# Two P V products of chunks 2 to 4 put directly behind each other, first W2 pieces and LayerNorm moved

## The chip, the cores and the metric

The kernel runs on one core of one Trainium2 chip. The metric is the device time of one execution in microseconds (us). A second measure is the span of the profiled execution: from its first to its last instruction. TensorE (PE in the profile; PEld for its weight loads) does the matrix products, VectorE (DVE), ScalarE (ACT) and GpSimd (POOL) the element-wise work, SyncE (SP) issues nearly all transfers.

## The reference

Two branches are computed from the same LayerNorm and added to the input:

```python
x = A_x                                   # [1, 2048, 576], bf16
xn = _layernorm(x, axis=-1)               # no scale, no shift, eps 1e-5
return x + _A_ref(xn, A_wqkv, A_wo) + _B_ref(xn, B_w1, B_w3, B_w2)
# _A_ref: 32 heads of 18, causal attention, each query sees the last 256 keys
#   scores = q k^T * 18**-0.5; p = softmax over the window; o = p v; o @ wo
# _B_ref: h = silu(xn @ w1) * (xn @ w3), 4608 wide; h @ w2
```

## The kernel before

The 2048 tokens are worked in four chunks of 512 (c = 0 to 3 in the code, chunks 1 to 4 in the text). W1, W3 and W2 are streamed from memory again for every chunk. The heads are taken in groups of four (g = 0 to 7) and pairs of groups (j = 0 to 3).

A chunk has these stages, one behind the other on TensorE:

1. **36 units** (u = 0 to 35; `unit_pairs`, L851). A unit makes 128 of the 4608 hidden features: nine steps (n = 0 to 8) of two matmuls of 64 rows each, one for W3 and one for W1, into two PSUM banks. `unit_tanh` (L866, ScalarE) and `unit_h` (L872, two VectorE instructions) then make `hT[:, u]`. Three pairs of banks (`JOBS`, dealt by `job()`) take turns, so unit u+3 writes where unit u was read.
2. Between the steps of the units stands attention: **score steps** (`score_step`, L1357: matmuls of L682, the exponential L691, masks L718) and **P V** (`pv`, L721: matmuls of 20 columns by 64 rows, L739). Chunk 1 does all eight groups here, chunks 2 to 4 groups 4 to 7 (pairs 2 and 3: 20 score steps, 96 matmuls for each P V). A P V writes two banks that `job()` gives it; `pv_out` (L799) turns them on VectorE, `o_scale` (L802) divides by the row sums, `o_turn` (L811) turns back, `o_pack` (L819) sends the result to `oT` by transfers.
3. Projections for the next chunk (L496), and then W2 with the scores and P V of groups 0 to 3 of the next chunk between (`w2_lanes`, L958). Chunk 4 has W2 and Wo alone instead (`p2_item`, L918).

The order on every engine is written out by the program. The planner has a clock that counts steps: a unit's step is 1, a score step 1, a P V `PV_COST` = 6.6 (L1288). `spaced_step` (L1368) spreads the score steps so that they end at `last`, which was the end of the units less 26 in chunks 2 to 4. In chunks 2 to 4 pair 2 has its P V behind unit `LATE_PV` = 20 (L1290, L1439), pair 3 behind unit 35 (L1496; in chunk 4 L1546, behind the first Wo matmuls of L846). In chunk 1 pairs 1 and 2 are at `JOINT` = (27, 6) (L1291, L1402), that is before the seventh step of unit 27: both P V run directly behind each other, in the two pairs of banks that unit 27 does not use. `calm` (L1305) keeps score steps out of the eight steps before it.

The probabilities of a score step lie in a slot. The first ten slots of chunks 2 to 4 (`early`, L1322) are borrowed: four are tiles 28 to 35 of `hT`, four the buffers of W2, two are tiles of `stage`. So the first four pieces of W2 (`load_w2`, L366) can be loaded only once the P V of pair 2 has read them. They are asked for behind units 25, 27, 29 and 31 in chunks 2 to 4 and behind units 27 to 30 in chunk 1.

LayerNorm of the next chunk's four token tiles is spread over the units by `near` (L1302): statistics at unit 8+4t, `ln_apply` at 10+4t, the transposing transfer `xn_send` at 11+4t. The rows of x are loaded at units 1, 2, 12 and 15 (L1307). W1 and W3 of later units are loaded in parts behind units 3, 7, ..., 23 (`owe_part`, L355): each part is issued when the step n = 3 or n = 8 of the unit after that is through; SP works its transfers in the order of the program.

Of the kernel before, what the change touches and what calls it, by code (L numbers as in the profile page):

```python
# [164 lines left out]
def bass_parallel_sum__sliding_block__glu_gated_swiglu__prompt_kernel(  # L165
# [21 lines left out]
    NF = F // 128  # L187
# [10 lines left out]
    with ExitStack() as es:  # L198
# [166 lines left out]

        def load_w2(upto):  # L366
            nonlocal n2fill
            if n2fill >= min(upto, NC * 2 * NFC):
                return
            s = n2fill % NW2  # L370
            m = n2fill % (2 * NFC)
            half, fc = divmod(m, NFC)
            n2fill += 1
            if n2fill <= (NC - 1) * 2 * NFC:
                if m < 16:
                    dst, f0, nf, d0, nd = w2_by(s, 128), m % 4 * 9, 9, m // 4 * 128, 128
# [6 lines left out]
            add("sp", lambda e: e.dma_start(  # L383
                w2[s][:], B_w2[fc * 512:(fc + 1) * 512, half * HD:(half + 1) * HD].rearrange("(fl p) d -> p fl d", p=128)),
                w=[("w2", s)], dma=f"w2_{s}")

# [911 lines left out]
        for c in range(NC):  # L1298
# [13 lines left out]
            npv = 3 if c == 0 else 1  # L1312
            total = 9 * NF + len(att) + npv * PV_COST
            start = 60 if c == 0 else 8
            last = total - AHEAD[c]
            nxt = soon = start
# [22 lines left out]
            def later(u, what):  # L1339
                side.setdefault(u, []).append(what)  # L1340
# [27 lines left out]
            def spaced_step():  # L1368
                nonlocal nxt, soon, clock
                score_step()  # L1370
                soon = clock + 7.5
                room = last - clock - PV_COST * (3 - next_pv) - 5 * sum(v > at_u for v in xt)
                nxt = max(soon, clock + room / max(1, len(att) - done))
                clock += 1
# [17 lines left out]
            for u in range(NF):  # L1392
# [44 lines left out]
                if u % 4 == 3 and u < (NF - 4 if c + 1 == NC else NF - 12) and (c or u != 15) or c and u == 0:  # L1437
                    owed += 2 if c or u >= 11 else 4
                if u == (LATE_PV if c else FIRST):  # L1439
                    j = next_pv  # L1440
                    assert j == j0 and clock >= pv_ready[j], (c, clock, pv_ready)
                    next_pv += 1
                    banks = job()
                    pv(c, j, banks)
                    clock += PV_COST
                    if c == 0:
                        release(j, None)
# [5 lines left out]
                    if j == 0:  # L1453
                        for n in range(7):
                            later(u + 5 + n, lambda n=n: o_rest(n, "sp"))
                unit_h(u, b0[0])
# [35 lines left out]
            assert done == len(att) and next_pv == 3, (done, next_pv)  # L1492
            assert clock + 2 >= pv_ready[3], (clock, pv_ready)
            if c + 1 < NC:
                banks = job()
                pv(c, 3, banks)  # L1496
                for g in range(GN, G):
# [10 lines left out]
                for m, what in enumerate(PROJ_LATER + [None]):  # L1508
                    got = proj_begin(c + 1, what) if what else proj_end()
                    if m == 0:  # L1510
                        xn_swap(c + 1, ("sp", "sp"))
                        if c == 0:
                            wo_late()
                        for u in sorted(side):
                            for do in side.pop(u):
                                do()
                        pv_out(banks[0], 0)
                        pv_out(banks[1], 1)
                        o_scale(0)
                    elif m == 1:  # L1520
                        o_turn(6, 0)
                        o_turn(6, 1)
                        o_scale(1)
                    elif m == 2:
                        o_turn(7, 0)
                        o_turn(7, 1)
# [3 lines left out]
                    elif got and got[0] == "8":  # L1530
                        new_k(2)
                    if m == 6:
                        o_pack(3, "sp")
# [11 lines left out]
            wo_rest(0, True, False)  # L1545
            pv(c, 3, banks)  # L1546
            for n, item in enumerate(p2_list(c)):
                p2_item(c, item, xs)
                if n == 3:
                    for u in sorted(side):  # L1550
                        for what in side.pop(u):
                            what()
                    pv_out(banks[0], 0)
                    pv_out(banks[1], 1)
                    o_scale(0)
                    o_turn(6, 0)
                    o_turn(6, 1)
                    o_scale(1)
                    o_turn(7, 0)
                    o_turn(7, 1)  # L1560
                    o_pack(3, "act")

# [30 lines left out]
```

## Time and profile before

| | us |
|---|---|
| three runs | 554.01, 554.99, 555.89; median 554.99 |
| the profiled execution | 554.85 |
| its span, first to last instruction | 553.1 |
| outside of the span | 1.75 |

A line of the profile's groups names line, engine, operation, what it writes and reads, the shapes and the count; behind the bar come busy time, the mean of one in ns, and the idle time ahead of them with what ended it. Matmuls overlap, so a mean of 376 ns of a matmul with 512 columns doesn't mean that it takes the engine that long: two on different rows of the array run beside each other, and the next pair starts 0.216 us later. In the timeline a row is a run of like instructions: start, length, and the count behind the x. "issue" is what the profile says where an engine stood idle and nothing that the profile knows held it back.

### The profile page before, as it was taken

To read this page: it belongs to the slowest core of one execution; us is meant where nothing else is said; L and a number is where in the kernel's file an instruction comes from. 1 tells how busy PE (TensorE), PEld (TensorE's weight loads), DVE (VectorE), ACT (ScalarE), POOL (GpSimd) and SP (SyncE) were. 2 spreads that over 40 slices of the span, in tenths; PEclk is the share of its full clock that TensorE was granted. 3 is DMA by queue.
4 is the path that set the end of the run, shared out by engine and by line. 5 is a ranking of instruction groups with operands and counts; after the bars stand their busy time and mean duration, and the time that the engine had idled before them with its cause. 6 is when DMAs were issued, how large, how long until landed. Compare 5 with 4: busy or idle time off the path is not lost.

```text
span 553.1 us, 17657 instructions
## 1 busy us (share of the span) xinstructions
PE 548.0 (99%) x7690; PEld 301.7 (55%) x7690; DVE 365.2 (66%) x745; ACT 294.0 (53%) x481; POOL 120.0 (22%) x281
## 2 busy tenths in 40 slices
PE   8999999999999999999999999999999999999998
PEld 4555445465564444455556444446555644545776
DVE  6566888845748888673764888866466686677211
ACT  6457776268825555536883555443787355554000
POOL 5513544200012423200001232320000222221000
PEclk9999999999999999999999999999999999999999
DMA  9997999849799997945989999793587999881552
GB/s 237 198 208 143 192 200 158 168 97 163 143 180 192 190 187 147 179 98 115 151 142 195 198 189 190 145 176 79 119 163 143 180 195 163 167 175 54 140 151 64
DMA packets 166070, 88.12 MB, mean 159 GB/s; under 512 B 101546, under 2 KB 163754, under 8 KB 165994
## 3 DMA queue, kind: packets, MB, share of 16 engines
q1 hardware_dynamic: 164514, 85.27, 82.2%
q10 hardware_dynamic: 1480, 1.73, 1.3%
q8 instruction: 60, 0.98, 0.8%
q14 instruction: 16, 0.13, 0.1%
HBM read 71.30 MB, written 2.36 MB: 133 GB/s over the span
## 4 chain that ended last, share of the span: by engine, by line
PE 97%; DMA 1%; SPq 1%; POOL 0%; issue 0%; DVE 0%
PE ps L860 51%; PE ps L1036 17%; PE ps L496 8%; PE ps L932 6%; PE ps L682 4%; PE ps L739 2%; PE ps L1086 2%; PE ps L1045 2%; PE ps L791 2%; PE ps L756 1%; DMA pt<-in_A_wqkv_dram 1%; PE ps L939 1%; SPq L1168 0%; PE ps L1096 0%; SPq L1172 0%
## 5 line engine op out<-in xcount | busy, mean ns | idle before, releaser
L860 PE MATMUL ps<-xnT,w 64*128 64x512 bf16 x1400 | 177.5, 376 | 0.0
L860 PE MATMUL ps<-xnS,w 64*128 64x512 bf16 x1120 | 148.6, 376 | 0.0
L875 DVE SCALAR_TENSOR_TENSOR gs<-thb,ps 128x512 bf16<-128x512 bf16 x144 | 97.9, 680 | 66.1 <-ACT thb L869 65.6
L869 ACT ACTIVATE thb<-ps 128x512 bf16<-128x512 f32 x144 | 85.6, 595 | 58.9 <-PE ps L860 57.7
L1036 PE MATMUL ps<-hT,w 32*128 32x512 bf16 x1728 | 106.9, 374 | 0.0
L860 PEld LDWEIGHTS ps<-xnT,w 64*128 64x128 bf16 x1400 | 67.2, 94 | 71.6
L878 DVE SCALAR_TENSOR_TENSOR hT<-gs,ps 128x512 bf16<-128x512 bf16 x144 | 98.9, 687 | 5.0
L860 PEld LDWEIGHTS ps<-xnS,w 64*128 64x128 bf16 x1120 | 53.7, 94 | 57.3
L1036 PEld LDWEIGHTS ps<-hT,w 32*128 32x128 bf16 x1728 | 57.3, 92 | 29.2 <-issue 1.4
L763 ACT ACTIVATE pt<-ps 128x512 bf16<-128x512 f32 x120 | 65.1, 594 | 7.7 <-PE ps L756 7.5
L691 ACT ACTIVATE pt<-ps 128x1024 bf16<-128x1024 f32 (+1 forms) x46 | 46.2, 1005 | 42.2 <-PE ps L682 42.2
L756 PE MATMUL ps<-qv,kn 18*128 18x384 bf16 (+2 forms) x288 | 54.6, 267 | 0.0
L806 POOL TENSOR_TENSOR oq<-uq,rden 128x288 bf16<-128x288 f32 x15 | 10.1, 672 | 198.7 <-DVE rden L805 198.7
L718 POOL TENSOR_TENSOR pt<-pt,mk 128x128 int32<-128x128 int32 (+1 forms) x82 | 33.0, 423 | 69.4 <-ACT pt L691 69.4
L771 DVE TENSOR_TENSOR pt<-pt,kv 128x256 int32<-128x256 int32 x96 | 31.4, 372 | 24.8 <-ACT pt L763 24.2
L496 PE MATMUL ps<-xnT,wp 64*128 64x512 bf16 (+1 forms) x360 | 38.2, 355 | 0.4 <-POOL mk L1270 0.4
L932 PE MATMUL ps<-w,hT 128*128 128x288 bf16 (+1 forms) x292 | 36.9, 284 | 0.0
L691 ACT ACTIVATE hT<-ps 128x1024 bf16<-128x1024 f32 (+1 forms) x20 | 20.0, 1002 | 31.5 <-PE ps L682 31.4
L756 PEld LDWEIGHTS ps<-qv,kn 18*128 18x128 bf16 x288 | 26.5, 93 | 15.0 <-DVE uq L800 0.8
L932 PEld LDWEIGHTS ps<-w,hT 128*128 128x128 bf16 x292 | 28.2, 98 | 7.3 <-issue 0.2
L682 PE MATMUL ps<-qv,kv 64*128 64x320 bf16 (+4 forms) x336 | 31.7, 258 | 0.0
L813 DVE STREAM_TRANSPOSE od<-oq 128x256 bf16<-128x256 bf16 x64 | 25.2, 424 | 6.3 <-POOL oq L806 6.3
(128 smaller groups left out, 522.8 us busy)
## 6 DMA issues: line engine op xcount, KB each, us to landing
w<-in_B_w_dram SPq DMA_DIRECT2D x60, 576.0 KB, 7.8
w<-in_B_w_dram SPq DMA_DIRECT2D x72, 288.0 KB, 4.3
w<-in_B_w_dram SPq DMA_DIRECT2D x12, 192.0 KB, 6.5
xp<-in_A_x_dram SPq DMA_DIRECT2D x4, 576.0 KB, 4.6
xnS<-xnT SPq DMA_DIRECT2D x8, 256.0 KB, 5.3
xp<-in_A_x_dram SPq DMA_DIRECT2D x14, 144.0 KB, 4.3
w<-in_B_w_dram SPq DMA_DIRECT2D x6, 320.0 KB, 4.8
oT<-od SPq DMA_DIRECT2D x52, 36.0 KB
```

The source lines that it names most:

```text
L496: op = add("pe", lambda e, out_=out_, st=st, mv=mv, n=n, r0=r0, first=first: e.matmul(out_, st, mv, start=first, stop=(part == 1 and n == ...
L682: add("pe", lambda e, r0=r0, out_=out_, kb=kb, q0=q0, nb=nb: e.matmul(out_, kb4[r0:r0 + 64, g - GN, kb + NV - NB, :] if kb < 0 else kv[r0: ...
L691: add("act", lambda e: e.activation(pt_slot(sl)[:, 0:w, :], PS[:, SC[0]:SC[1] + 1, 0:w].rearrange("p r q -> p q r"), ACT.Exp, scale=scale) ...
L718: add("pool", lambda e, vb=vb, mm=mm: e.tensor_tensor(vb, vb, mm, ALU.mult), r=(key if n == 0 else []) + ["mk"], **{"w" if n == 0 else "j" ...
L756: add("pe", lambda e: e.matmul(PS[:, b, c0:c0 + nb * 128], kn[32 * a:32 * a + Dh, g, W + 128 * jb:W + 128 * jb + 128], qv[32 * a:32 * a + ...
L763: add("act", lambda e: e.activation(head_of(sl, p), PS[:, b, :], ACT.Exp, scale=scale), r=[("ps", b)], **{"j" if p else "w": pt_keys(sl)})
L860: op = add("pe", lambda e, n=n, r0=r0, r=r, k=k, src=src: e.matmul(PS[:, b0 + r, :], wt[r0:r0 + 64, k, fl * 128:(fl + 1) * 128], src, star ...
L869: add("act", lambda e: e.activation(th[i][:], PS[:, bg, :], ACT.Tanh, scale=0.5), r=[("ps", bg)], w=[("th", i)])
L875: add("dve", lambda e: e.scalar_tensor_tensor(out=gs[i][:], in0=th[i][:], scalar=1.0, in1=PS[:, bg, :], op0=ALU.add, op1=ALU.mult), r=[("t ...
L878: add("dve", lambda e: e.scalar_tensor_tensor(out=hT[:, u, :], in0=gs[i][:], scalar=0.5, in1=PS[:, bu, :], op0=ALU.mult, op1=ALU.mult), r= ...
L932: add("pe", lambda e: e.matmul(bank, hT[:, f, tt * 128:(tt + 1) * 128], w2[sl][:, k, n0:n1], start=first, stop=(c + 1 == NC and half == 1 ...
L1036: add("pe", lambda e, b=b, rows=rows, wt=wt, fl=fl, k=k, a=a, first=first: e.matmul(PS[:, b, :], wt[rows, fl, :], hT[rows, k, :], start=fi ...
```

## The change

In chunks 2 to 4 the P V of pairs 2 and 3 both go to (27, 6), directly behind each other, as chunk 1 has it for its pairs 1 and 2. The P V behind unit 20, the one behind unit 35 and in chunk 4 the one ahead of W2 go away, with the steps that followed them (`pv_out`, `o_scale`, `o_turn`, `o_pack`), which now follow behind units 27 to 33. The 20 score steps end at clock 246 (`ALL_DONE`) and so stand closer together; the eight steps ahead of the joint place stay free of them in every chunk. W2's first four pieces are asked for behind units 28 to 31 in all chunks, and each issue waits for the last matmul of its unit. LayerNorm of the next chunk is two units sooner, its third and fourth loads of x come at units 9 and 13. The number of matmuls stays.

```diff
-        def load_w2(upto):
+        def load_w2(upto, after=()):
...
-                    w=[("w2", s)], dma=f"w2_{s}")
+                    w=[("w2", s)], after=after, dma=f"w2_{s}")
...
-        LATE_PV = 20
         JOINT = (27, 6)
-        AHEAD = [40, 26, 26, 26]
+        AHEAD, ALL_DONE = 40, 246
...
-                    {t: tuple(8 + 4 * t + k for k in (0, 2, 3)) for t in range(4)})
+                    {t: tuple(6 + 4 * t + k for k in (0, 2, 3)) for t in range(4)})
...
-            calm = range(9 * JOINT[0] + JOINT[1] - 8, 9 * JOINT[0] + JOINT[1]) if c == 0 else ()
+            calm = range(9 * JOINT[0] + JOINT[1] - 8, 9 * JOINT[0] + JOINT[1]) 
...
-            loads = {8: (2,), 17: (3,)} if c == 0 else {1: (0,), 2: (1,), 12: (2,), 15: (3,)}
+            loads = {8: (2,), 17: (3,)} if c == 0 else {1: (0,), 2: (1,), 9: (2,), 13: (3,)}
...
-            last = total - AHEAD[c]
+            last = total - AHEAD if c == 0 else ALL_DONE
...
-                    if c == 0 and (u, n) == JOINT:
-                        ja = 1
+                    if (u, n) == JOINT:
+                        ja = j0 or 1
...
-                if u == (LATE_PV if c else FIRST):
+                if c == 0 and u == FIRST:
...
-                if u in (range(27, 31) if c == 0 else range(LATE_PV + 5, LATE_PV + 12, 2)):
-                    load_w2(c * 2 * NFC + 4)
+                if u in range(28, 32):
+                    load_w2(c * 2 * NFC + 4, (op,))
...
             if c + 1 < NC:
-                banks = job()
-                pv(c, 3, banks)
+                if c == 0:
+                    banks = job()
+                    pv(c, 3, banks)
...
             wo_rest(0, True, False)
-            pv(c, 3, banks)
             for n, item in enumerate(p2_list(c)):
                 p2_item(c, item, xs)
                 if n == 3:
                     for u in sorted(side):
                         for what in side.pop(u):
                             what()
-                    pv_out(banks[0], 0)
-                    pv_out(banks[1], 1)
...
-                    o_pack(3, "act")
```

More of the change, by code (lines that the diff above doesn't have):

```diff
@@ L384, in load_w2 @@
                 w2[s][:], B_w2[fc * 512:(fc + 1) * 512, half * HD:(half + 1) * HD].rearrange("(fl p) d -> p fl d", p=128)),
-                w=[("w2", s)], dma=f"w2_{s}")
+                w=[("w2", s)], after=after, dma=f"w2_{s}")
         def ln_stats(t, s, part):
@@ L1311, in bass_parallel_sum__sliding_block__glu_gated_swiglu__prompt_kernel @@
                 loads[4] = (0, 1)
[L1312 to L1313 removed]
+            total = 9 * NF + len(att) + 3 * PV_COST
             start = 60 if c == 0 else 8
[L1315 removed]
+            last = total - AHEAD if c == 0 else ALL_DONE
             nxt = soon = start
@@ L1371, in spaced_step @@
                 soon = clock + 7.5
-                room = last - clock - PV_COST * (3 - next_pv) - 5 * sum(v > at_u for v in xt)
+                room = last - clock - (PV_COST * (3 - next_pv) if c == 0 else 0) - 5 * sum(v > at_u for v in xt)
                 nxt = max(soon, clock + room / max(1, len(att) - done))
@@ L1452, in bass_parallel_sum__sliding_block__glu_gated_swiglu__prompt_kernel @@
                     later(u + 4, lambda j=j: o_pack(j, "sp"))
-                    if j == 0:
-                        for n in range(7):
-                            later(u + 5 + n, lambda n=n: o_rest(n, "sp"))
+                    for n in range(7):
+                        later(u + 5 + n, lambda n=n: o_rest(n, "sp"))
                 unit_h(u, b0[0])
@@ L1516, in bass_parallel_sum__sliding_block__glu_gated_swiglu__prompt_kernel @@
                                 do()
+                    if c == 0 and m == 0:
                         pv_out(banks[0], 0)
@@ L1519, in bass_parallel_sum__sliding_block__glu_gated_swiglu__prompt_kernel @@
                         o_scale(0)
-                    elif m == 1:
+                    elif c == 0 and m == 1:
                         o_turn(6, 0)
@@ L1523, in bass_parallel_sum__sliding_block__glu_gated_swiglu__prompt_kernel @@
                         o_scale(1)
-                    elif m == 2:
+                    elif c == 0 and m == 2:
                         o_turn(7, 0)
@@ L1531, in bass_parallel_sum__sliding_block__glu_gated_swiglu__prompt_kernel @@
                         new_k(2)
-                    if m == 6:
+                    if c == 0 and m == 6:
                         o_pack(3, "sp")
```

13 lines of the change are left out of this document (3 added, 10 removed).

## The prediction

> **What bounds the kernel now.** I read the page first: span, busy shares, clock, the chain that ended last, the queues.
>
> ```profile
> span 553.1 us, 17657 instructions
> PE 548.0 (99%) x7690; PEld 301.7 (55%) x7690; DVE 365.2 (66%) x745; ACT 294.0 (53%) x481; POOL 120.0 (22%) x281
> ...
> PEclk9999999999999999999999999999999999999999
> ...
> q8 instruction: 60, 0.98, 0.8%
> ...
> PE 97%; DMA 1%; SPq 1%; POOL 0%; issue 0%; DVE 0%
> ```
>
> TensorE is the bound from end to end, at full clock, and 97% of the chain is its own work. So nothing is won by relieving another engine; the change counts by what it takes from TensorE's stream, and by any hole it tears into it. Next the chain in order of time, for how dense a stretch of bare units is, and the windows of the P V line (L739) alone, one window for each P V of the kernel:
>
> ```profile
> 231.62 6.04 PE ps L860 x56
> ```
>
> ```profile
> core 0: us, PE busy (x) PEld busy (x), PEclk, DMA share, GB/s
> 53.00:55.50 2.50, 1.26 (x72) 0.84 (x72) 1.00 0.45 66
> 82.00:85.00 3.00, 1.98 (x144) 1.61 (x144) 1.00 1.22 150
> 101.50:104.00 2.50, 1.05 (x72) 0.78 (x72) 1.00 1.18 205
> 205.00:208.00 3.00, 1.40 (x96) 1.08 (x96) 1.00 1.27 159
> 237.00:240.00 3.00, 1.37 (x96) 1.07 (x96) 1.00 0.83 152
> 341.00:344.00 3.00, 1.64 (x96) 1.08 (x96) 1.00 0.87 104
> 373.00:376.00 3.00, 1.37 (x96) 1.07 (x96) 1.00 0.76 138
> 477.00:480.00 3.00, 1.38 (x96) 1.10 (x96) 1.00 0.83 177
> 509.00:512.00 3.00, 1.37 (x96) 1.07 (x96) 1.00 0.03 5
> ```
>
> 56 matmuls in 6.04 us are 28 pairs at 0.216 us: no holes. Each matmul comes with one weight load, so a stretch of units takes 112 instructions in 6.04 us, 18.5 per us. Of the P V, like ones cost 1.37 to 1.40 us, but that of chunk 3 at 341 us costs 1.64 and the first of chunk 1 1.26 against 1.05. The timeline of TensorE around these two shows why:
>
> ```profile
> 54.13 0.22 PE L739 MATMUL ps<-hT,va 64*20 64x128 bf16 x2
> 54.64 0.23 PE L739 MATMUL ps<-hT,va 64*20 64x128 bf16 x2 [0.30 <-issue]
> ...
> 342.14 0.30 PE L739 MATMUL ps<-w,va 64*20 64x256 bf16 x4
> 342.17 0.59 PE L739 MATMUL ps<-stage,va 64*20 64x256 bf16 x4
> 342.49 0.29 PE L739 MATMUL ps<-w,va 64*20 64x256 bf16 x4
> ```
>
> Both P V break off in the middle of a row of like matmuls, for 0.3 us, with no semaphore to blame ("issue"; in the second 0.3 us lie within the row at 342.17). What ended these waits is in the page's q8. Its 0.98 MB are 60 packets of 16,384 bytes, and 7690 matmuls and 7690 weight loads at 64 bytes make the same 0.98 MB: q8 fetches TensorE's instructions, 256 in a packet. Count the instructions between the two breaks:
>
> ```profile
> 54.60:342.47 287.87, 287.82 (x4324) 153.51 (x4323) 208.08 (x438) 168.47 (x276) 66.62 (x159) 1.00 0.93 165
> 54.60:161.70 107.10, 107.06 (x1778) 59.60 (x1777) 76.26 (x168) 67.71 (x114) 26.71 (x63) 1.00 0.91 161
> 54.60:297.42 242.82, 242.78 (x3798) 132.01 (x3797) 171.29 (x366) 143.93 (x242) 52.21 (x123) 1.00 0.90 160
> 54.60:433.40 378.80, 378.74 (x5818) 204.31 (x5817) 266.41 (x564) 220.14 (x370) 77.72 (x183) 1.00 0.89 160
> ```
>
> The first row has 4324 + 4323 = 8647; the views leave out TensorE's separate waiting instructions, of which the trace holds 57 here. Together 8704 = 34 x 256, exactly. Both breaks fall on the first instruction of a fetched block. The trace's packet records (no view groups them) give the rest. Left are the packets whose blocks were late, right all block boundaries that fell into or just behind a P V, with the packet that was fetched from there:
>
> ```
> block began   its packet (took)          boundary   next packet (took)  after
>  54.64        51.79 (1.35), end 53.14      54.64      59.55 (1.32)       4.91
> 342.48       339.65 (1.42), end 341.07     83.55      85.29 (1.31)       1.74
>                                           102.18     104.09 (1.41)       1.91
>                                           206.33     210.37 (1.41)       4.04
>                                           238.26     240.57 (0.95)       2.32
>                                           342.48     345.96 (1.34)       3.48
>                                           374.43     376.59 (0.95)       2.16
>                                           510.47     511.41 (1.42)       0.94
> ```
>
> One block is fetched ahead, never two: with a boundary the next packet is asked for, it waits among the other transfers (0.94 us in the window at 509, where DMA is 0.03 busy, up to 4.91), takes 0.95 to 1.42, and its instructions run 1.41 to 1.50 us after its end. Units use a block up in 256 / 18.5 = 13.8 us, so there this is hidden. In a P V it is not.
>
> **The change part by part.** *The joint P V.* Chunk 1 already has its like:
>
> ```profile
> 82.62 1.05 PE L739 MATMUL ps<-pt,va 64*20 64x320 bf16 x72
> ...
> 84.53 0.36 PE L682 MATMUL ps<-qv,kv 64*128 64x320 bf16 x4
> ```
>
> 288 instructions in 1.91 us. By the windows the joint pair is busy 1.98 against 2 x 1.05 apart, 0.12 less. The six single P V of chunks 2 to 4 sum to 8.53; three joint ones of 2 x 1.37 - 0.12 = 2.62 make 7.86. **Gain 0.7 us**, chunk 3's break of 0.27 in it.
>
> But a joint P V here has 2 x 96 matmuls and 192 weight loads: 384 instructions at 192 / 1.30 = 148 per us, more than one block. If its first 128 instructions hold a boundary, the whole next block is used up inside, in 256 / 148 = 1.73 us, and the least that the table allows for a fetch is 0.94 + 0.95 + 1.41 = 3.3.
>
> Where do the boundaries fall? Nothing changes TensorE's count ahead of chunk 2. The second row has 3555 instructions from a block's start to unit 0 of chunk 2, and 25 waiting ones: 3580. To (27, 6) come 27 units of 36, six steps of 4, all 20 score steps (192 instructions) and 8 waits for W1 and W3: 1196. 4776 = 18 x 256 + 168, so the next boundary is 88 instructions into the joint P V, and the one behind it at 344, both inside. Chunk 3: 7595 + 50 + 1196 = 8841 leaves 119 and 375, both inside. Chunk 4: 11635 + 75 + 1196 = 12906 leaves 150 and 406, the second 22 behind the end. An error of three waiting instructions moves none of them across.
>
> The price. How late the packet starts I take from the nearest row, 1.74 at 83.55: chunk 1's own joint P V, the same place in the unit loop, a part of W3 and W1 asked for behind step (24, 8) still landing.
>
> ```profile
> w<-in_B_w_dram SPq DMA_DIRECT2D x60, 576.0 KB, 7.8
> w<-in_B_w_dram SPq DMA_DIRECT2D x72, 288.0 KB, 4.3
> ```
>
> The median of 7.8 us from issue to landing, against some 5.3 us of units from (24, 8) to the joint place, says that this part lands 2.5 us into the joint P V in every chunk. So the packet leaves at a fixed time, and a later boundary waits less: 1.74 in chunk 2, 0.21 less (31 / 148) in chunk 3, 0.42 less in chunk 4. With 1.31 (that packet's own transfer) and 1.45 (the middle of 1.41 and 1.50) the block is there 4.50, 4.29 and 4.08 us after the boundary. It is wanted after 1.73, 1.73 and, in chunk 4, 234 / 148 + 22 / 18.5 = 2.77 us. **Stalls 2.8 + 2.6 + 1.3 = 6.7 us.** All work of TensorE stands behind them. Bounds: with the least of each, 1.6 + 1.6 + 0.5 = 3.7; with the late rows (4.04 + 1.41 + 1.45), 5.2 + 5.2 + 4.1 = 14.5.
>
> The Trainium skill ("Runtime: NRT & Kernel Launch", "Instruction fetch mechanics") also has refills of 16 KiB blocks of 256 instructions while the page before runs, but calls the boundary's cost mostly hidden. By that the sum would be the gain of 0.7 alone. The trace agrees on the blocks and disagrees on the hiding, with its two breaks of 0.3 us; the page makes a rival below.
>
> *The steps behind the P V.* Eight `o_turn` and four `pv_out` now crowd into units 27 to 33. Chunk 1 does the same with score steps besides, and the cover is the third pair of banks:
>
> ```profile
> 83.83 0.72 DVE L800 STREAM_TRANSPOSE uq<-ps 128x512 f32<-128x512 f32 x1 [0.36 <-PE ps L739]
> 84.47 0.67 DVE L800 STREAM_TRANSPOSE ofin<-ps 128x512 f32<-128x512 f32 x1
> 85.07 0.21 DVE L805 RECIPROCAL rden<-uq 128x16 f32<-128x16 f32 x1
> 85.20 1.25 DVE L800 STREAM_TRANSPOSE pt<-ps 128x512 f32<-128x512 f32 x2
> ```
>
> The first two banks are free 1.31 us after their P V ends, at some 2.9 us of the joint P V; unit 28 wants them at 2.62 + 3 x 0.216 = 3.3. Cost 0, at most 0.4 each if VectorE comes late. ScalarE's score steps come closer, one in 11 clock steps of 0.216 us:
>
> ```profile
> L869 ACT ACTIVATE thb<-ps 128x512 bf16<-128x512 f32 x144 | 85.6, 595 | 58.9 <-PE ps L860 57.7
> ...
> L691 ACT ACTIVATE pt<-ps 128x1024 bf16<-128x1024 f32 (+1 forms) x46 | 46.2, 1005 | 42.2 <-PE ps L682 42.2
> ```
>
> 1.0 us in 2.4 beside 0.6 of a unit's 1.94 fill it to 0.73, and chunk 1 has 32 such steps in its units without a hole: 0.
>
> *W2's pieces.* SP issues four loads of 4.3 us behind units 28 to 31; the waits hold up only what stands behind on SP, `o_pack` and x of chunk 4, which nobody wants before W2. In chunk 4 the last piece is wanted some 14 us after its issue: 0. If they came 2 us late it would be 2.
>
> *LayerNorm sooner*: no change of work; x's loads at units 9 and 13 stand behind parts of W1 and W3 (7.8 us), but the statistics come five units later (5 x 1.94 = 9.7 us and 0.2 for each score step): 0, up to 0.5 if VectorE stands waiting for them.
>
> *Chunk ends*: a P V less ahead of the projections and of W2 is in the gain.
>
> Sum: -0.7 + 6.7 = **+6.0** (from +3.0 to +13.8). The profiled execution took 554.85 (553.1 and 1.75 around it), the median of the runs is 554.99; on the median I get 560.9.
>
> **The rivals.** (1) *The fetch is hidden after all*: a second block could be on its way while the slow units run, and the joint P V has no break. For it: chunk 1's joint P V has none, with 288 instructions. Against: there the boundary lay 0.9 us in (83.55 against 82.62), and the next one, 256 later, behind its end; and each of the 60 packets came singly, about its own boundary. It would give 555.0 - 0.7 = 554.3, not slower. (2) *Banks late at units 28 to 30* through the crowded VectorE, with hidden fetches: 3 x 0.4 - 0.7 gives 555.5, decided by when the second `pv_out` ends. Against it, the rows above. (3) *The clock falls in the breaks.* A break longer than some 3 us could cost TensorE its clock; the program's first ten matmuls of 512 columns run at half:
>
> ```profile
> 1.24 4.17 PE L1160 MATMUL ps<-oq 128*128 128x512 bf16 x10 [1.24 <-DVE oq L1154]
> ```
>
> 0.42 us each where 0.216 is usual, so each falling would cost about half of such a stretch, 2 us: in all three 560.9 + 6 = 567. Against it, the longest break in the trace, 0.3 us, shows nothing of it either way. The Trainium skill ("TensorE: Matmul & The Clock Gate", "What's actually happening") states an idle window of about 3.4 us for it; my breaks are shorter, those of the upper bound are not.
>
> **How the numbers follow.** The forecast has 0.82, rival 1 has 0.09, rival 2 0.03, rival 3 (or equally late fetches) 0.06. The predicted time is 560.9. The range: the forecast's own bounds are 558 to 569 (554.99 + 3.0 and + 13.8); fetches in this place are likely nearer the row at 83.55 than the late ones, so I end at 565.5, and go down to 556.5, since the runs of one kernel lie up to 1 us from their median; outside are the two rivals below and the late end, 0.2 together. This measurement tells about 0.3% (1.7 us) from no change: slower by that 0.88, within it 0.1, faster 0.02 (three P V have no more than 0.7 to give).
>
> **What would show it.** In the profile after: within L739 at unit 27 of chunks 2 and 3 a break of 2 to 3 us with "issue" ahead of it, some 40 and 10 instructions before the joint P V ends; in chunk 4 one of about 1 us just behind its end, in L860; none in chunk 1. The window of L739 there reads about 5.4, 5.2 and 2.6 us busy and idle together. Everything else on TensorE keeps its 0.216 us. The prediction is wrong if these P V run through in 2.6 us, if the breaks stand elsewhere or are ended by a semaphore, or if units 28 to 30 wait for VectorE.

## The result, and the profile after

| | before, us | changed, us |
|---|---|---|
| median of six runs each | 555.36 | 560.35 |
| lowest and highest | 554.01, 555.89 | 558.01, 561.08 |
| the profiled execution | 554.85 | 560.37 |
| its span | 553.1 | 558.6 |

The ratio is 1.0084, with a 95% interval of 1.0058 to 1.0109: the change makes the kernel slower by 0.84%. The prediction was 560.9.

The page of the changed kernel first: span, busy shares, the granted clock, the shares of the chain that ended last.

```profile
span 558.6 us, 17660 instructions
...
PE 549.3 (98%) x7690; PEld 302.2 (54%) x7690; DVE 366.6 (66%) x745; ACT 294.0 (53%) x481; POOL 120.6 (22%) x281
...
PEclk9999999999999999899999999999999999999999
...
q8 instruction: 60, 0.98, 0.8%
...
PE 96%; DMA 1%; issue 1%; SPq 1%; DVE 0%
```

As many matmuls as before, and a span 5.5 us longer. TensorE is still the bound, but "issue" now has 1% of the chain, and one slice of the clock shows an 8. What TensorE stood waiting for, summed over the changed kernel (total, times, longest):

```profile
PE ps L739 <- issue: 4.3, 3, 2.2
PE ps L1160 <- DVE oq L1154: 1.2, 1, 1.2
PE ps L860 <- issue: 0.6, 1, 0.6
```

The wait at L1160 is at the start of the program and as long before. New are 4.3 us of "issue" inside P V (0.3 us before) and 0.6 us just behind one. No row names VectorE ahead of a unit, and none names W2. TensorE's timeline of the changed kernel shows where they lie, in chunks 1 to 4:

```profile
82.75 0.31 PE L739 MATMUL ps<-w,va 64*20 64x320 bf16 x3
83.81 0.31 PE L739 MATMUL ps<-w,va 64*20 64x320 bf16 x1 [0.75 <-issue]
...
221.35 1.10 PE L739 MATMUL ps<-pt,va 64*20 64x320 bf16 x76
224.67 0.66 PE L739 MATMUL ps<-pt,va 64*20 64x64 bf16 x20 [2.22 <-issue]
225.26 1.04 PE L860 MATMUL ps<-xnS,w 64*128 64x512 bf16 x4
226.09 2.15 PE L860 MATMUL ps<-xnT,w 64*128 64x512 bf16 x10
228.07 1.03 PE L860 MATMUL ps<-xnS,w 64*128 64x512 bf16 x8
...
360.70 1.32 PE L739 MATMUL ps<-pt,va 64*20 64x320 bf16 x91
363.40 0.29 PE L739 MATMUL ps<-pt,va 64*20 64x256 bf16 x5 [1.38 <-issue]
...
499.52 0.81 PE L860 MATMUL ps<-xnT,w 64*128 64x512 bf16 x6
500.94 0.60 PE L860 MATMUL ps<-xnT,w 64*128 64x512 bf16 x4 [0.60 <-issue]
```

In chunk 2 TensorE breaks off with 20 matmuls of the joint P V left, that is 40 instructions; in chunk 3 with 5 left, 9 instructions (the weight load of the first had gone through); in chunk 4 in the first units behind it. These are the places that the prediction counted out: 344 of 384, 375 of 384, and 22 behind the end. The break of 0.75 us in chunk 1 was not predicted. And behind the break of chunk 2 something else is wrong: the ten matmuls at 226.09 take 2.15 us, where the eight at 228.07 take 1.03. The windows of TensorE around it give its granted clock (window and length in us, TensorE's busy time and matmuls, granted clock, DMA share, GB/s):

```profile
221.00:223.00 2.00, 1.45 (x132) 1.00 0.47 76
223.00:225.00 2.00, 0.33 (x20) 0.87 0.00 0
225.00:227.00 2.00, 2.00 (x26) 0.50 0.04 8
227.00:229.00 2.00, 2.00 (x18) 0.77 0.00 0
```

The trace's clock record has one stretch at 0.5 here, from 224.49 to 227.91. TensorE worked again from 224.67, so that this took half of 3.24 us: 1.6 us.

The packet records of TensorE's instruction fetches (no view groups them), for the block that came late in each P V; "in" is the place of the boundary within the joint P V, in instructions:

```
chunk  in    boundary before   packet left (after)  took   block began (after its end)
 1     158     76.89            80.78 (3.89)        1.40    83.81 (1.63)
 2     344    220.79           221.82 (1.03)        1.40   224.67 (1.45)
 3     375    360.24           361.05 (0.82)        1.13   363.40 (1.22)
 4     406    497.50           498.71 (1.20)        0.96   500.93 (1.27)
```

Each break ends 1.2 to 1.6 us after its packet has landed. That breaks fall on block boundaries holds in all 13 traces of this document: between 20 us and the last matmul TensorE has 24 idle stretches of 0.19 us or more that no semaphore ends. Number its records from 0 and divide by 256, and the instruction that ends such a stretch leaves the same remainder, 193, all 24 times.

What each chunk lost is read from when TensorE began its first unit (L860 in the timeline), and for the last chunk from its last matmul:

```
                      before    changed   later by   lost in the chunk ahead
unit 0 of chunk 1      21.80     21.51     -0.29
unit 0 of chunk 2     161.74    161.96      0.22      0.51
unit 0 of chunk 3     297.47    301.31      3.84      3.62
unit 0 of chunk 4     433.46    438.38      4.92      1.08
last matmul           550.29    555.84      5.55      0.63
```

The joint P V that ran undisturbed, chunk 4's, took 2.54 us:

```profile
496.40:499.20 2.80, 2.54 (x192) 2.22 (x192) 1.00 0.45 74
```

Three of those against 8.53 before save 0.9. Breaks of 2.22 + 1.38 + 0.60 + 0.75 = 4.95 and the clock's 1.6, less this 0.9, less the break of 0.3 at 54 us, which this execution does not have, and less the 0.29 at the start make 5.1, where the span grew by 5.5. The rest lies in the breaks: one costs about 0.2 us more than its idle time says. That of chunk 1, 0.75 us idle, put TensorE back by 1.03 against the profile before, and at 54 us, where only the profile before has a break, of 0.30 us idle, the changed kernel made up 0.51.

### The profile page after: what moved, and what is told of

Read it like the earlier page. It is cut to its first block, busy times and chain, and to the rows that moved or that the text cites. A ratio compares the mean times of both kernels' runs of the same rounds, so it can differ in the third digit from the quotient of the medians.

```text
span 558.6 us, 17660 instructions
## 1 busy us (share of the span) xinstructions
PE 549.3 (98%) x7690; PEld 302.2 (54%) x7690; DVE 366.6 (66%) x745; ACT 294.0 (53%) x481; POOL 120.6 (22%) x281
## 4 chain that ended last, share of the span: by engine, by line
PE 96%; DMA 1%; issue 1%; SPq 1%; DVE 0%
PE ps L860 50%; PE ps L1036 17%; PE ps L496 8%; PE ps L932 6%; PE ps L682 4%; PE ps L739 2%; PE ps L1086 2%; PE ps L1045 2%; PE ps L756 2%; PE ps L791 2%; DMA pt<-in_A_wqkv_dram 1%; PE ps L939 1%; SPq L1168 0%; PE ps L1096 0%; SPq L1172 0%
## 5 line engine op out<-in xcount | busy, mean ns | idle before, releaser
L860 PE MATMUL ps<-xnT,w 64*128 64x512 bf16 x1400 | 178.6, 378 | 0.6 <-issue 0.6
L860 PE MATMUL ps<-xnS,w 64*128 64x512 bf16 x1120 | 147.1, 377 | 0.0
L860 PEld LDWEIGHTS ps<-xnT,w 64*128 64x128 bf16 x1400 | 67.2, 94 | 70.1 <-issue 2.5
L860 PEld LDWEIGHTS ps<-xnS,w 64*128 64x128 bf16 x1120 | 54.3, 94 | 60.3 <-issue 0.7
L806 POOL TENSOR_TENSOR oq<-uq,rden 128x288 bf16<-128x288 f32 x12 | 8.1, 674 | 206.9 <-DVE rden L805 206.9
L990 DVE TENSOR_TENSOR thb<-ps,thb 128x512 f32<-128x512 f32 x24 | 16.6, 692 | 18.5 <-ACT thb L987 17.9
```

The costliest lines, as they stand in the source:

```text
L860: op = add("pe", lambda e, n=n, r0=r0, r=r, k=k, src=src: e.matmul(PS[:, b0 + r, :], wt[r0:r0 + 64, k, fl * 128:(fl + 1) * 128], src, star ...
```

## The experiments

The theory: the breaks are instruction fetches, set by where the block boundaries fall in a stretch that uses 148 instructions per us. Rivals: the data, the banks or the order around unit 27 make TensorE wait at a fixed place; or the other parts of the change (W2, LayerNorm) cost what was lost.

### Boundaries moved by fulfilled waits

```diff
+                    for _ in range(o.pad):
+                        e.wait_ge(sems["pool"], 1)
...
+        PADS = [0, 176, 31, 31]
...
+                    more = PADS[c] * u // 26 - PADS[c] * (u - 1) // 26 if n == 2 and 0 < u < 27 else 0
+                    op.pad = 2 * more + (more > 0)
```

The changed kernel, with waits on TensorE strewn over units 1 to 26, ahead of a unit's third step, for a semaphore that GpSimd has raised long before: they hold nothing up. Two of them make one instruction of the stream, so that 176, 31 and 31 instructions are added in chunks 2, 3 and 4. Work and order stay.

> The changed kernel with TensorE's instruction stream made longer by waits that are fulfilled long before (one instruction each): 176 in the units of chunk 2, 31 in those of chunks 3 and 4. Matmuls, data and their order stay. A block boundary then falls 167 instructions into each of the three joint P V, the next one 39 behind its end. Theory (instruction fetch): the block behind is wanted 2.1 + 1.5 = 3.6 us after the boundary, and in the changed kernel's profile packets left 0.8 to 1.2 us after it and were usable 2.2 to 2.9 us later (3.1 to 3.9 in all), so breaks shrink from 2.4, 1.6 and 1.0 us to 0 to 0.3 each, and the time to 0.7 us under the kernel before, 554.7 against 555.4 (554 to 556). Rival (the second P V waits for something of its own: masks, banks, transposes): the breaks stay on the same matmuls, 558 to 561. Rival (waiting instructions themselves cost time): the breaks go, but units with waits take longer than 0.216 us a pair, up to 238 x 0.02 = 5 us.

Measured: 555.14 us (median of 12), ratio 1.0013 (1.0003 to 1.0023). Nearly all of the loss is gone, though nothing was done to P V, W2 or LayerNorm; the 0.7 us under the kernel before that were expected did not come. The profiled execution was the longest of the twelve, 558.05 us. Its timeline, chunk 2 and then the whole tail of the joint P V of chunks 3 and 4:

```profile
223.64 0.29 PE L742 MATMUL ps<-stage,va 64*20 64x256 bf16 x4 [2.67 <-issue]
...
360.85 1.36 PE L742 MATMUL ps<-pt,va 64*20 64x320 bf16 x96
362.14 0.61 PE L863 MATMUL ps<-xnS,w 64*128 64x512 bf16 x4
...
496.29 1.37 PE L742 MATMUL ps<-pt,va 64*20 64x320 bf16 x96
497.59 0.61 PE L863 MATMUL ps<-xnS,w 64*128 64x512 bf16 x4
```

(L742 is L739 and L863 is L860; the edit adds three lines.) In chunks 3 and 4 the last 96 matmuls run through. In chunk 2 the break is there, at the new boundary, 168 in: its packet, wanted since 214.91, left at 220.84, while W3 and W1 parts issued at 213.37 and 214.67 were landing at 219.72 and 223.62. So the good position does not rid this place of its risk, it only gives the packet more time. Against the profile before, chunk 3 is 0.55 us shorter here (its break of 0.3 before is in that) and chunk 4 0.17: that is what the joint P V gains where nothing breaks.

### A shift by 60, in chunk 2 alone

The same edit with `PADS = [0, 60, 0, 0]`.

> The changed kernel with 60 fulfilled waits in the units of chunk 2 alone: boundaries then fall 27, 58 and 89 instructions into the joint P V of chunks 2, 3 and 4, the next ones at 283, 314 and 345, all inside. Theory (instruction fetch): the breaks move by exactly 60 instructions towards the front; the one of chunk 4, which lay 22 instructions behind the end, moves into the P V line and grows from 0.8 us of lost time to 1.5 to 2.6; all three are 1.5 to 2.6 us, longer where transfers still land at the boundary; time 559.5 to 563. Rival (something of the second P V's own): the breaks stay on the same matmuls with the same lengths, 558 to 561.

Measured: 561.57 us (median of 4), ratio 1.0134 (1.0118 to 1.015). The timeline of this kernel at the three breaks:

```profile
223.44 0.72 PE L742 MATMUL ps<-pt,va 64*20 64x128 bf16 x50 [1.76 <-issue]
224.09 0.61 PE L863 MATMUL ps<-xnS,w 64*128 64x512 bf16 x4
...
362.70 0.63 PE L742 MATMUL ps<-pt,va 64*20 64x320 bf16 x35 [3.43 <-issue]
363.26 0.60 PE L863 MATMUL ps<-xnS,w 64*128 64x512 bf16 x4
...
497.42 1.10 PE L742 MATMUL ps<-pt,va 64*20 64x320 bf16 x76
500.15 0.44 PE L742 MATMUL ps<-pt,va 64*20 64x64 bf16 x20 [1.63 <-issue]
```

Left in the joint P V are 50, 35 and 20 matmuls, where the changed kernel had 20, 5 and none. Counted in the trace, the breaks stand at 284, 315 and 346 instructions in place of 344, 375 and 406: all three have moved forward by 60, also in chunks 3 and 4, where nothing but the count ahead of them was changed. A wait for data, a bank or a weight would have stayed at its matmul. Chunk 4's break, now inside the P V, grew from 0.60 to 1.63. The one of chunk 3, 3.43 us, is longer than the 1.5 to 2.6 expected: its packet left 2.45 us after the boundary.

### W2's pieces and LayerNorm without the joint P V

```diff
-                    {t: tuple(8 + 4 * t + k for k in (0, 2, 3)) for t in range(4)})
+                    {t: tuple(6 + 4 * t + k for k in (0, 2, 3)) for t in range(4)})
...
-            loads = {8: (2,), 17: (3,)} if c == 0 else {1: (0,), 2: (1,), 12: (2,), 15: (3,)}
+            loads = {8: (2,), 17: (3,)} if c == 0 else {1: (0,), 2: (1,), 9: (2,), 13: (3,)}
...
-                if u in (range(27, 31) if c == 0 else range(LATE_PV + 5, LATE_PV + 12, 2)):
-                    load_w2(c * 2 * NFC + 4)
+                if u in range(28, 32):
+                    load_w2(c * 2 * NFC + 4, (op,))
```

The kernel before with these two parts of the change, and then with the LayerNorm part alone (the first two pairs of lines).

> The kernel before with the other parts of the change alone: W2's first pieces behind units 28 to 31, each waiting for the last matmul of its unit, and LayerNorm two units sooner with its loads of x at units 9 and 13; the P V stay behind units 20 and 35. Theory: these parts cost nothing, 555.4 like the kernel before (within 0.3%), units at 0.216 us a pair, the same single P V. Rival (the loads or LayerNorm cost part of the 5 us): 557 to 560, with waits of TensorE on VectorE in units 6 to 22 or on W2 at the start of chunk 4's last stage.

> The kernel before with LayerNorm two units sooner and its loads of x at units 9 and 13, nothing else. The run of the two moved parts together was 0.2% slower, with a break of 2.0 us in chunk 3's P V at unit 20, on the same boundary as the break of 0.3 us before. Theory A (LayerNorm's transposing transfers now go between the two parts of W3 and W1, so that these and the instruction packet behind them land later): the same here, a packet 1.5 to 2 us later than before in chunk 3, a break of 1.5 to 2.5 us there, ratio 1.001 to 1.003. Theory B (W2's waiting issues do it): a break of 0 to 0.5 us as before, ratio 0.999 to 1.001.

Measured: both parts 555.51 us, ratio 1.0021 (1.0009 to 1.0032); LayerNorm alone 555.54 us, ratio 1.0025 (1.0013 to 1.0037). So W2's part costs nothing that these two runs could tell (each is known to 0.12%), and LayerNorm, put down at 0, about 0.2%, some 1.2 us. In the profile of both parts (span 555.0) most of the time stands in one row of TensorE's waits, a single P V of chunk 3:

```profile
PE ps L739 <- issue: 1.7, 1, 1.7
```

It is the break that was 0.30 us before, on the same boundary, with its packet leaving at 341.53 where it left at 339.65. The transposing transfer of LayerNorm that SP issued at 331.90, right ahead of the last two parts of W3 and W1 there, now stands at 328.43, and the next one at 335.94, right behind them, where it stood at 339.92; a part issued at 333.31 landed at 344.06 (10.75 us), where one issued at 333.84 had landed at 342.81 (8.97). That the order made it land later, and the packet leave later, is argued, not shown. In the profiled execution of LayerNorm alone (span 553.1), with the same order, that packet left at 339.61, no later than before, and the break was 0.5 us, not the 1.5 to 2.5 expected, so that its 0.2% is not shown by its own trace.

### The two P V two units apart

```diff
+        APART = (27, 29)
...
-                    if (u, n) == JOINT:
-                        ja = j0 or 1
+                    if c == 0 and (u, n) == JOINT:
+                        ja = 1
...
-                if c == 0 and u == FIRST:
+                if u in APART if c else u == FIRST:
...
-                    for n in range(7):
+                    for n in range(7 if c == 0 else 0):
```

In chunks 2 to 4 pair 2's P V goes behind unit 27 and pair 3's behind unit 29; all else as in the changed kernel. In the first of the two forms a turn of pair 2 reads what pair 3's first division has already written, so its output is another, with the same work; in the second both last turns follow two units behind the P V.

> The changed kernel with the two P V of chunks 2 to 4 not directly behind each other: pair 2 behind unit 27, pair 3 behind unit 29, 72 instructions of units between; score steps, W2's loads and LayerNorm as in the changed kernel. Boundaries fall 75, 106 and 137 instructions behind the start of pair 2's P V, so the next ones, 256 later, lie 67, 98 and 129 instructions into pair 3's. Theory (a joint P V uses a block up faster than the next is fetched): between the two boundaries now lie 0.8 + 3.9 + 0.5 = 5.2 us in chunk 2 (as much in the others) against 3.1 to 3.9 that a fetch takes there, so no breaks at these places; the time is that of the kernel before within 0.3%, 554 to 556. Rival (more instructions late in the chunk, or the crowded VectorE): breaks or waits of TensorE of 1 us and more at units 27 to 33, 557 to 560.

> The kernel with the two P V apart (pair 2 behind unit 27, pair 3 behind unit 29), with the steps behind pair 2 mended: its last two turns both come two units behind it, so that they are through before pair 3's first division overwrites what they read. Otherwise the changed kernel. Theory: as with the first form, no breaks at the six P V of chunks 2 to 4, 0.998 to 1.001 of the kernel before. Rival: the mended turns make units 29 and 30 wait for VectorE, 0.5 to 1 us in each chunk, 1.002 to 1.005.

Measured: 554.16 us, ratio 0.9992 (0.9978 to 1.0006), and 555.09 us, ratio 1.0003 (0.9992 to 1.0014). The timeline of TensorE in the second form, chunk 2, from unit 28 on:

```profile
221.56 1.04 PE L860 MATMUL ps<-xnT,w 64*128 64x512 bf16 x8
222.43 1.03 PE L860 MATMUL ps<-xnS,w 64*128 64x512 bf16 x8
223.29 1.24 PE L860 MATMUL ps<-xnT,w 64*128 64x512 bf16 x10
224.38 1.03 PE L860 MATMUL ps<-xnS,w 64*128 64x512 bf16 x8
225.24 0.38 PE L860 MATMUL ps<-xnT,w 64*128 64x512 bf16 x2
225.55 1.37 PE L739 MATMUL ps<-pt,va 64*20 64x320 bf16 x96
226.85 1.04 PE L860 MATMUL ps<-xnT,w 64*128 64x512 bf16 x8
```

Four us of units between the two P V are enough: no P V of chunks 2 to 4 breaks. So it is the direct succession that costs, not the late place.

### Later and aligned

```diff
-        JOINT = (27, 6)
-        AHEAD, ALL_DONE = 40, 246
+        JOINT_AT = [(27, 6), (30, 6), (30, 6), (30, 6)]
+        PADS = [0, 67, 31, 31]
+        AHEAD, ALL_DONE = 40, 273
...
-                if u in range(28, 32):
+                if u in (range(28, 32) if c == 0 else range(31, 35)):
```

The joint P V at (30, 6) in chunks 2 to 4, W2's pieces behind units 31 to 34, waits of 67, 31 and 31 instructions so that the boundary again lies some 168 in. Units 28 and 29 then write the tiles of `hT` in which pair 2's probabilities lie, before its P V reads them: the P V takes part of its input from other data, with the same work.

> The changed kernel with the joint P V of chunks 2 to 4 at (30, 6), score steps done by clock 273, W2's first pieces behind units 31 to 34, and fulfilled waits in the units (67 in chunk 2, 31 in 3 and 4) so that a boundary falls 167 instructions into each joint P V. Theory (instruction fetch): by then the last part of W3 and W1 has landed, so the packet asked for 8 us ahead is there in time, and the next boundary has 3.6 us against 3.1 to 3.4 of a fetch on idle queues; no breaks in chunks 2 to 4, the gain of 0.7 us shows: 0.998 to 1.000 of the kernel before. Rival (late packets whatever the place): breaks of 1 to 3 us stay, 556 to 558. Rival (W2 later): TensorE waits for W2 at the start of chunk 4's last stage, 1 to 3 us.

Measured: 557.23 us (median of 5), ratio 1.0051 (1.0038 to 1.0063). The waits of TensorE in this kernel (L742 and L881 are L739 and `unit_h`, L935 is a matmul of W2):

```profile
PE ps L742 <- DVE hT L881: 2.5, 3, 0.8
PE ps L935 <- DMA w<-in_B_w_dram: 1.5, 1, 1.5
```

No "issue" here: the position keeps its promise in all three chunks. But TensorE stands 0.8 us ahead of each joint P V until VectorE has written the tiles of `hT` that it reads, which no expectation had, and 1.5 us for a piece of W2 in chunk 4, which the second rival had. The place at unit 27 is thus not to be moved back freely; three units later W2 is late.

### The changed kernel once more

> The changed kernel as it is, beside the one with the P V apart on the same chip, for the direct difference and a second profile of its three breaks. Theory: breaks on the same instructions (344 and 375 into the joint P V of chunks 2 and 3, 22 behind the end in chunk 4) of 1.6 to 3 us, 1.6 to 3 us and 0.7 to 2 us; 1.008 to 1.012 of the kernel before, some 5 us over the P V apart. Whether the clock falls is open: it fell behind breaks of 2.2 and 2.7 us of idle time and not behind ones of 1.4 to 1.8 and 3.4.

Measured: 560.47 us (median of 4), ratio 1.0106 (1.0076 to 1.0135). Its profiled execution (558.97, span 557.3) breaks at the same three instructions:

```profile
224.35 0.43 PE L739 MATMUL ps<-pt,va 64*20 64x64 bf16 x20 [2.26 <-issue]
224.72 0.61 PE L860 MATMUL ps<-xnS,w 64*128 64x512 bf16 x4
225.16 1.03 PE L860 MATMUL ps<-xnT,w 64*128 64x512 bf16 x8
...
362.02 0.29 PE L739 MATMUL ps<-pt,va 64*20 64x256 bf16 x5 [1.82 <-issue]
362.25 0.61 PE L860 MATMUL ps<-xnS,w 64*128 64x512 bf16 x4
```

Here the clock did not fall: eight matmuls take 1.03 us behind a break of 2.26 us. Of the ten executions of the changed kernel, five have a mean granted clock of 1.000 and took 558.01 to 560.33, on average 558.9; five have 0.997 or less and took 560.37 to 562.59, on average 561.3. So without the clock's fall the change costs about 3.9 us against 555.0, and executions with it are some 2.4 us longer. In the trace above the fall itself took 1.6, so the rest of the 2.4 need not be the clock's. The execution of 560.33 stands apart from the four others at 1.000 (558.01 to 558.97); a trace without clock records is given as 1.000 too, so that it may belong to the other half.

### LayerNorm back in its old units

The LayerNorm edit above taken back in the two-units-apart form and in the one with moved boundaries, and the former once more beside them.

> The kernel with the two P V two units apart, but with LayerNorm and the loads of x in the units of the kernel before. Theory (LayerNorm's part costs 0.2 to 0.25 %, which the two-units-apart form has paid and won back elsewhere): 0.997 to 0.9985 of the kernel before, some 553.5 to 554.2 us, and faster than the form with the early LayerNorm by about 1 us. Rival (the 0.2 % comes from how score steps and LayerNorm fall together in the kernel before alone, or is a matter of where blocks of instructions begin): no difference from the form with the early LayerNorm, 1.000.

> The changed kernel with the fulfilled waits that shift the block boundaries, and LayerNorm and the loads of x in the units of the kernel before. TensorE's instruction stream is the same, so the boundaries stay at 167. Theory: 0.999 of the kernel before (1.0013 less 0.2 to 0.25 %). Rival: 1.001, as with the early LayerNorm.

> The two-units-apart form with the early LayerNorm once more, beside the two others on one chip: 1.0003 again, within 0.0015.

Measured, in this order: 554.70 us, ratio 1.000 (0.9988 to 1.0012); 556.03 us, 1.002 (1.0011 to 1.003); 554.20 us, 0.998 (0.9968 to 0.9992). The theory of a fixed price of 0.2% falls: with the P V apart or aligned, the early LayerNorm is, if anything, the better one. The waits of the aligned form with the old LayerNorm show where TensorE stands there (L863 is a unit's matmul):

```profile
PE ps L863 <- issue: 2.0, 2, 1.2
```

These breaks lie 40 instructions behind the joint P V of chunks 2 and 3. Their packets left 2.28 and 1.92 us after the boundary, against 1.06 and 0.90 with the early LayerNorm. In chunk 2 the two profiles can't be compared so simply: with the early LayerNorm the boundary itself came behind the break of 2.67 us, which the old one does not have (its packet ahead left 0.18 us before the boundary, not 5.93 after it). There a transposing transfer, which stood at 209.21 in that form, now stands at 213.37, right ahead of the last parts of W3 and W1, whose issues move from 213.37 and 214.67 to 214.63 and 216.07. That LayerNorm costs or helps by where its transfers put the weights beside the packets agrees with this, but it rests on one profile of each form.

No form beats the kernel before by more than can be told: the one with two units between has 0.9992, 1.0003 and 0.998 in its three measurements, and the two of the same kernel (1.0003 and 0.998) lie so far apart that their intervals only just touch.

## Why the prediction was right, and where it was not

**The mechanism and the places: right.** The count of instructions put the breaks at 344, 375 and 406, and there they are, in both profiles of the changed kernel. Shift, alignment and separation answer as the fetch demands: the shift by 60 moved all three breaks by 60 instructions. The rival "the fetch is hidden" is refuted, and with it, for this stretch, the sentence of the Trainium skill ("Runtime: NRT & Kernel Launch", "Instruction fetch mechanics") that the cost of a boundary is mostly hidden: hidden it is in the units, while at 148 instructions per us it was 2.2 us. One reading of the prediction was too narrow: "with a boundary the next packet is asked for". A packet left about its boundary, in the profile before from 1.71 us ahead of it (504.2) to 4.91 behind. The other rival, late banks, did not come: no unit waits for VectorE, nor for ScalarE, whose score steps stand closer together.

**The size of the stalls: too large.** The step that failed is "How late the packet starts I take from the nearest row, 1.74 at 83.55". Measured were 1.03, 0.82 and 1.20 us (1.26, 0.98 and 0.86 in the second profile) instead of 1.74, 1.53 and 1.32. Landing and the time until the block could be used were close (0.96 to 1.40 and 1.22 to 1.45, set at 1.31 and 1.45). From the boundary to the block's first instruction it was 3.88, 3.16 and 3.43 us, set at 4.50, 4.29 and 4.08; chunk 3 went below the 3.3 that was taken as the least. So the breaks were 2.22, 1.38 and 0.60, 4.2 us in place of 6.7, and 4.8 with the 0.2 us that each costs beyond its idle time. The part of W3 and W1 did land 2.5 us into the joint P V, as worked out (2.67 and 2.51 in chunks 2 and 3, 1.89 in chunk 4), but the packet left about 1 us before that in chunks 2 and 3, so that it did not wait for this landing. That it waits less, the later the boundary, holds in the second profile and not in the first. The windows of the joint P V came to 5.1, 4.15 and 2.54 us where 5.4, 5.2 and 2.6 were announced.

**The clock: a rival that came true by half.** "My breaks are shorter" than the idle window was the reason to leave it out of the sum. The clock fell after a break of 2.22 us, for 3.4 us, and it was below 1.000 in half of the executions. The executions with it are some 2.4 us longer, which nearly fills up what the stalls were too large by. The reason failed because the length of the break alone does not decide (see the last section). That the median met the forecast within 0.6 us is luck, owed to these errors of opposite sign: without the clock's fall the changed kernel takes 558.9, not 560.9 (the prediction's own sum, 554.99 + 6.0, is 561.0).

**Chunk 1: wrong.** "None in chunk 1" overlooked that its boundary, 158 instructions into the joint P V, had a packet that came just in time: in the profile before it ended at 81.89, and the block began 1.66 us later, at 83.55, without a wait. A packet that left 1.1 us later after its boundary made a break of 0.75. In the other kernels the breaks of chunk 1 come and go, from none to 0.75 us, though its code ahead of them is the same. Against it the break at 54 us was gone, so that chunk 1 lost 0.51 us in all.

**The gain: right in kind.** 0.9 instead of 0.7, by the one undisturbed joint P V (2.54, set at 2.62). No run has the gain alone; in the aligned run the two chunks without a break were shorter by 0.55 and 0.17.

**W2: right**, at 0, and the warning held: asked for three units later, TensorE waits 1.5 us. **LayerNorm: mis-sized.** "No change of work" was true, and x's loads are not late; but moving it made the kernel before 0.2% slower, and the two other forms no slower. That its transfers do this by changing when weights and packets land is argued above. That term is not one number, and what it is in the changed kernel itself was not tried.

## What to carry to other kernels

A dense stretch of small matmuls is bound by its instructions too: count them per us, and count where the blocks of 256 begin. Where a joint P V broke, the block was there 3.2 us after the boundary before it at best, and up to 8.7 us with weights landing, so a stretch that uses 256 instructions in 1.73 us must end, or be broken up by slower work, before the second boundary. Here some 240 instructions far ahead of such stretches were worth 0.7%, and a comparison of two orders should be read with that in mind.

## What the runs showed of the hardware that was not expected

- The clock falls after some breaks of TensorE and not after others of the same or greater length. It fell after 2.22 us and after 2.67 us (the run with moved boundaries), and not after 2.26, 1.82 or 3.43 us. Behind the break of 3.43 us, in chunk 3 of the shift by 60, the units run at their usual pace (that trace has no clock record):

```profile
363.70 1.24 PE L863 MATMUL ps<-xnT,w 64*128 64x512 bf16 x10
364.78 1.03 PE L863 MATMUL ps<-xnS,w 64*128 64x512 bf16 x8
```

The run with the moved boundaries, behind its break in chunk 2:

```profile
221.00:223.00 2.00, 0.00 (x0) 1.00 0.33 52
223.00:225.00 2.00, 1.36 (x68) 0.74 0.03 8
225.00:227.00 2.00, 2.00 (x66) 0.50 0.00 0
227.00:229.00 2.00, 2.00 (x20) 0.91 0.03 8
```

The Trainium skill ("TensorE: Matmul & The Clock Gate", "What's actually happening") has an idle window of about 3.4 us that runs freely and does not begin anew with a kernel. The clock records agree with a window that runs by itself: in the changed kernel's trace the stretches between two changes are 218.45, 3.41 and 331.09 us, that is 64, 1 and 97 times 3.413, and in eight others the one stretch at full clock is 160 to 162 times 3.413. The first rise lies anywhere from 4.10 to 6.79 us, so that the windows fall differently on the program in each execution. One wholly idle window, as that page has it, was not needed. Cut into windows of 3.413 us at the clock's changes, TensorE's time shows this:

```
run                  window            idle in it   clock at its end
changed              221.08 to 224.49     2.04       falls
moved boundaries     220.55 to 223.97     2.67       falls
changed once more    219.44 to 222.85     0.76       stays    (the break of 2.26 us
                     222.85 to 226.26     1.50       stays     lies across both)
                     359.38 to 362.80     1.83       stays
later and aligned    551.89 to 555.30     2.16       falls    (end of the program)
```

In the ten traces that have clock records, all eleven falls, nine of them behind the end of the program's matmuls, end a window with 2.04 us of idle time or more, and no window after the first rise with 1.83 us or less ends in a fall. So what these traces show is that the idle time within one such window counts, with the limit between 1.83 and 2.04 of 3.41 us, and that a break can escape by lying across two windows. No run varied this on purpose.

- An instruction packet leaves later where much is being transferred: up to 6.9 us after its boundary (LayerNorm alone, 212.78 after 205.89). Over all traces, where the DMA engines were less than 0.1 busy from 0.5 us ahead of the boundary to 2 us behind it, the packet left from 2.0 us ahead of it to 1.3 us behind it, with a median of 0.94 behind; where they were over 0.9 busy the median was some 1.6. That it queues behind the weights is a reading of this. How long it waits changes from execution to execution, and with it the breaks.
- Some 240 instructions of fulfilled waits, strewn over the units, cost TensorE nothing that shows: eleven of the twelve executions of that kernel took 553.78 to 556.5 us.
